# A recurrent cross-attention block and a token-mixing MLP: one fixed order for all engines in place of a scheduled order

## The chip, the cores and the metric

The kernel runs on one core of one Trainium2 chip. A core has a matrix engine (PE, with its weight loads shown as PEld), a vector engine (DVE), a scalar engine (ACT), GpSimd (POOL) and a queue engine (SP). Each works through a queue of its own in order, and engines wait for each other by semaphores. Loads and stores go through 16 DMA engines, fed from the queues of SP, ACT and POOL. Matmul results land in PSUM, which has eight banks of 2 KB per partition; DVE and ACT copy them from there to SBUF. The metric is the device time of one execution in microseconds; less is better.

## The reference

The inputs are x (8 batches, 8 heads, 512 tokens, 64 features) and a state (32 rows for each batch and head). Each head's tokens attend to its state rows, and its state rows attend to its tokens. The two results, 512 + 32 = 544 rows, go through a linear token-mixing step.

```python
scores = scale * x @ state.T;  a = softmax(scores);   xread = a @ state
scores2 = scale * state @ x.T; a2 = softmax(scores2); sread = a2 @ x
y = concatenate([xread, sread], axis=2)        # (B, H, 544, 64) -> (B, 544, 512)
wq = y @ w_q;  wk = y @ w_k                    # 512 -> 64
mixed = (scale * wq @ wk.T) @ y                # over the 544 tokens
out = maximum(mixed, 0) @ w_out                # 512 -> 512, float32
```

## The kernel before

The work is cut by batch. For each batch b the steps are these (line numbers are those of the listing at the end of this section; the names in brackets are the short names that the new order uses for the same step):

- `s_xT` (xT): 16 PE transposes of x, in two halves of 8 into `xT_ps`; DVE copies each half out (L147, L152).
- `s_pt` (pt, exp, rs, rinv, A): the scores, 16 matmuls into `pt_ps` (L161); ACT takes the exponential `E` (L169); DVE sums and inverts (L174, L176); POOL multiplies into `A` (L178).
- `s_stbd`: POOL spreads the state rows of a batch to a block-diagonal tile `stbd`, two multiplications by a mask (L190).
- `s_at` (at, ate): 8 transposes of `A`, copied to `AT` by DVE (L203, L207).
- `s_srd` (srd, sums, srn, sbd): the state's reading, 32 small matmuls of 32 output rows and 8 for the sums (L216, L226); DVE normalises to `srn`; POOL spreads it to `sbd` (L242).
- `s_srT`, `s_wqk` (srT, wq, wks, wk): the two projections, from `AT` and from `srT` (L264, L273, L285, L294), copied out as `wq` by ACT and `wk` by DVE. The products with the state, `sw`, are made once at the start (L124).
- `s_g`, `s_v` (g, v): two small contractions that leave `V` in SBUF (L310, L326, L330, L338).
- `s_mix`, `s_mix_s` (mix0, mix1, mixs): the mixing, 8 matmuls of 64 rows and 4 short ones (L348, L367); the rectified results `rmix` are written by ACT (first half, L357) and DVE (second half, L359), `rmix_s` by ACT.
- `s_fin_mm` (fin0 to fin3): the output projection, 16 matmuls of 512 columns (L382). Two quarters share one tile of two banks, which ACT copies to `ost` (L393) and SP stores. `s_fin_s` (fs) does the same for the state rows of four batches at once (L412).

The matmul tiles differ in shape: most are 128 by 128, but `srd` and the state part of `wk` have 32 output rows (128*32 in the profile's rows), `wq` has 64 (128*64), `mix` and `mixs` contract over 64 rows (64*128), and `sw` is 64*32. PE runs each shape in a tiling mode of its own.

The code is written as a pipeline of three stages over ten rounds: batch i is in its front (xT, pt, srd), batch i-1 in its middle (at, wqk, g, v), batch i-2 in mix and fin. The framework's scheduler then moves instructions within what the tile pools and dependences allow. PSUM is split into pool `psA` (three tiles of two banks) and pool `psB` (two tiles of one bank). At the start x of batch 0 is loaded as float32 by four DMAs on ACT's queue and cast on DVE and ACT; the other batches and `w_out` are loaded and cast in flight by eight DMAs that POOL issues one after the other (L88 to L92); state and `w_q`, `w_k` come on SP's queue.

Of the kernel before, what the change touches and what calls it, by code (L numbers as in the profile page):

```python
# [14 lines left out]

@with_exitstack
def kernel(
# [9 lines left out]
    nc = tc.nc  # L27

    B, H, S, D = x.shape
    NS = state.shape[2]  # L30
    DM = H * D
# [11 lines left out]
    xin = ctx.enter_context(tc.tile_pool(name="xin", bufs=1))  # L43
# [5 lines left out]
    x_bf = [xin.tile([128, H, NC * D], BF, name=f"x_bf{b}") for b in range(B)]  # L49
    x_f0 = xin.tile([128, H, NC * D], FP, name="x_f0")  # L50
    st_f = const.tile([128, B, 2, D], FP, name="st_f")
    st_bf = const.tile([128, B, 2, 2, D], BF, name="st_bf")
    stT = const.tile([128, B, H, 2, NS], BF, name="stT")
    w_f = const.tile([128, NP, 2, DH], FP, name="w_f")
# [13 lines left out]
    st_src = state.rearrange("b (r q) n d -> (q n) (b r) d", r=2)  # L68
    nc.sync.dma_start(out=st_f[:, 0], in_=st_src[:, 0:2])
# [3 lines left out]
    wsrc = [w.rearrange("(r q d) j -> r d q j", r=2, q=NP) for w in (moe_w_q, moe_w_k)]  # L73
# [5 lines left out]
    nc.gpsimd.memset(stT[:, 1:B].bitcast(FP), 0.0)  # L79
    nc.vector.memset(stT[:, 0].bitcast(FP), 0.0)  # L80
    nc.vector.memset(mask, 0.0)
    nc.vector.memset(ones, 1.0)
    nc.vector.memset(warm, 0.0)
    nc.scalar.activation(out=warm, in_=warm, func=AF.Exp)
    for q in range(NP):
        nc.vector.memset(mask[NS * q : NS * q + NS, q : q + 1], 1.0)

    nc.gpsimd.dma_start(out=x_bf[1], in_=xsrc(1, 0, H))  # L88
    for b in range(2, B):
        nc.gpsimd.dma_start(out=x_bf[b], in_=xsrc(b, 0, H))  # L90
        if b == 2:
            nc.gpsimd.dma_start(out=w_o, in_=moe_w_out.rearrange("(k p) e -> p k e", p=128))  # L92

    def setup_st(b0, b1):
        n = b1 - b0
        nc.vector.tensor_copy(  # L96
            out=st_bf[:, b0:b1],
            in_=st_f[:, b0:b1, :, None, :].to_broadcast((128, n, 2, 2, D)),
        )
        ps = psB.tile([128, n, 2, HN], BF, name="stT_ps", tag="psB")  # L100
        for b in range(b0, b1):
            for r in range(2):
                nc.tensor.transpose(  # L103
                    out=ps[:, b - b0, r, :], in_=st_bf[:, b, r, :, :], identity=ident
                )
        for b in range(b0, b1):
            for c2 in range(2):
                rows = slice(64 * c2, 64 * c2 + 64)
                src = ps[rows, b - b0].rearrange("p r (q n) -> p (r q) n", q=NP)
                if c2 == 0:  # L110
                    nc.vector.tensor_copy(out=stT[rows, b, :, c2, :], in_=src)
                else:
                    nc.scalar.copy(out=stT[rows, b, :, c2, :], in_=src)

    def setup_w():
        nc.scalar.copy(out=w_qk[:, :, 0:2, :], in_=w_f)
        nc.vector.tensor_copy(out=w_qk[:, :, 2, :], in_=w_f[:, :, 1, :])

    def setup_sw(g):
        ps = psA.tile([128, 2, B // 2, 2 * DH], FP, name="sw_ps", tag="psA")  # L120
        for bb in range(B // 2):
            for q in range(NP):
                for r in range(2):
                    nc.tensor.matmul(  # L124
                        out=ps[NS * q : NS * q + NS, r, bb, :],
                        lhsT=stT[64 * r : 64 * r + 64, g * (B // 2) + bb, NP * r + q, r, :],
                        rhs=w_qk[64 * r : 64 * r + 64, q, 0:2, :],
                        start=True,
                        stop=True,
                    )  # L130
        src = ps.rearrange("p r b j -> p b r j")
        bs = slice(g * (B // 2), (g + 1) * (B // 2))
        dst = sw[:, bs].rearrange("p b r t j -> p b r (t j)")
        if g == 0:
            nc.scalar.copy(out=dst, in_=src)
        else:
            nc.vector.tensor_copy(out=dst, in_=src)

    live = [dict() for _ in range(B)]

    def s_xT(b):
        L = live[b]
        ps = psA.tile([128, NC // 2, H, 128], BF, name="xT_ps", tag="psA")
        xT = work.tile([128, NC // 2, H, 128], BF, name="xT")
        for u in range(2):
            for h in range(H):
                nc.tensor.transpose(  # L147
                    out=ps[:, u, h, :],
                    in_=x_bf[b][:, h, 128 * u : 128 * u + 128],
                    identity=ident,  # L150
                )
            nc.vector.tensor_copy(out=xT[:, u], in_=ps[:, u])  # L152
        L["xT"] = xT

# [359 lines left out]
```

## Time and profile before

| what | before |
|---|---|
| median of three runs (lowest, highest) | 116.53 us (115.98, 117.35) |
| the profiled execution's own time | 116.32 us |
| its span in the trace | 114.5 us |
| matmuls recorded on PE | 1321 |
| read from and written to HBM | 10.22 MB, 8.91 MB |

The profiled execution lies 0.2 us under the median; 1.8 us of it lie outside the span. A busy share in the profile counts a matmul from its start until its last result has left the array. A stream of matmuls overlaps these passages, so a PE that is shown 95% busy need not be streaming all of that time. The granted clock is the share of TensorE's full speed.

### The profile page before, as it was taken

Reading aid. Unit: us, or ns where it says so; the run is one execution under the profiler, and the core shown is the slowest. Engines: PE = TensorE matmul, PEld = TensorE weight load, DVE = VectorE, ACT = ScalarE, POOL = GpSimd, SP = SyncE. Lnnn points to the kernel's source line nnn. Section 1 sums busy time; section 2 is a strip of 40 time slices with the busy share of each in tenths; the row PEclk is TensorE's granted clock in tenths of the full one; section 3 lists DMA queues with packets and bytes.
Section 4 is the critical chain, followed back from the end, with each engine's and each line's share of the span. In section 5 each row is a group of like instructions: output and inputs, shape, how many; then the busy total and the mean of one; then the engine's idle time right before and its main releaser. Section 6 shows DMA issues by size and latency. Waiting matters only on the chain. (4 is left out here: it accounts for less than half of the span.)

```text
span 114.5 us, 3055 instructions
## 1 busy us (share of the span) xinstructions
PE 87.3 (76%) x1321; PEld 54.8 (48%) x1336; DVE 58.2 (51%) x117; ACT 47.3 (41%) x70; POOL 43.3 (38%) x55
## 2 busy tenths in 40 slices
PE   0223398684979999999999989989998997949600
PEld 0002375684655657366555726565674554524200
DVE  1325565658423727852953694296449435344200
ACT  0522449030163346438442644544573454480210
POOL 8995000583990390086058107700630640000000
PEclk9999999999755999999999999999999999999995
DMA  1999999999900044040404404052332224044381
GB/s 39 290 287 183 197 204 197 199 197 198 126 0 0 6 183 182 7 186 6 183 0 189 180 3 167 24 192 77 157 154 74 104 84 183 0 203 187 87 298 48
DMA packets 14933, 15.13 MB, mean 132 GB/s; under 512 B 3656, under 2 KB 12360, under 8 KB 14920
## 3 DMA queue, kind: packets, MB, share of 16 engines
q0 software_dynamic: 7808, 4.19, 26.3%
q1 hardware_dynamic: 5736, 9.18, 22.5%
q10 hardware_dynamic: 1376, 1.57, 4.6%
q8 instruction: 10, 0.16, 0.6%
q14 instruction: 3, 0.02, 0.1%
HBM read 10.22 MB, written 8.91 MB: 167 GB/s over the span
## 5 line engine op out<-in xcount | busy, mean ns | idle before, releaser
L382 PE MATMUL fin_ps<-w_o,rmix 128*128 128x512 bf16 x113 | 32.7, 386 | 4.9 <-ACT rmix L357 2.2
L178 POOL TENSOR_TENSOR A<-E,rinv 128x1024 bf16<-128x1024 bf16 x8 | 15.3, 1912 | 47.3 <-DVE rinv L176 28.8
L393 ACT COPY ost<-fin_ps 128x1024 f32<-128x1024 f32 x14 | 14.2, 1012 | 10.8 <-PE fin_ps L382 10.4
L147 PE MATMUL xT_ps<-ident,x_bf 128*128 128x128 bf16 x128 | 13.0, 252 | 6.1 <-ACT x_bf L429 3.0
L382 PEld LDWEIGHTS <-rmix 128*128 128x128 bf16 x128 | 10.7, 99 | 14.4 <-issue 2.8
L152 DVE COPY xT<-xT_ps 128x1024 bf16<-128x1024 bf16 x16 | 11.0, 686 | 12.4 <-PE xT_ps L147 12.4
L147 PEld LDWEIGHTS <-x_bf 128*128 128x128 bf16 x128 | 9.7, 112 | 9.3 <-ACT x_bf L429 3.5
L169 ACT ACTIVATE E<-pt_ps 128x1024 bf16<-128x1024 f32 x8 | 8.2, 1023 | 11.9 <-PE pt_ps L161 11.9
L359 DVE TENSOR_SCALAR rmix<-mix_ps 128x1024 bf16<-128x1024 f32 x8 | 9.7, 1218 | 6.5 <-PE mix_ps L348 6.5
L174 DVE TENSOR_REDUCE rsum<-E 128x32 f32<-128x1024 bf16 x8 | 9.7, 1213 | 2.8 <-ACT E L169 2.8
L338 ACT ACTIVATE V<-v_ps 128x512 bf16<-128x512 f32 x8 | 4.8, 597 | 14.9 <-PE v_ps L330 14.9
L242 POOL TENSOR_TENSOR sbd<-srn,mask 128x256 bf16<-128x256 bf16 x16 | 9.5, 612 | 1.8 <-DVE srn L237 1.7
L190 POOL TENSOR_TENSOR stbd<-st_bf,mask 128x256 bf16<-128x256 bf16 x16 | 9.4, 611 | 0.0
L357 ACT ACTIVATE rmix<-mix_ps 128x1024 bf16<-128x1024 f32 x8 | 8.2, 1028 | 1.3 <-PE mix_ps L348 1.3
L103 PE MATMUL stT_ps<-ident,st_bf 128*128 128x128 bf16 x16 | 2.6, 305 | 6.9 <-DVE st_bf L96 4.0
L302 DVE CAST wk<-wk_ps 128x384 bf16<-128x384 f32 x8 | 4.4, 548 | 6.6 <-PE wk_ps L294 6.6
L348 PE MATMUL mix_ps<-wq,V 64*128 64x256 bf16 x64 | 6.7, 291 | 1.2 <-ACT V L338 0.7
L161 PE MATMUL pt_ps<-stT,xT 128*128 128x64 bf16 x128 | 6.9, 212 | 0.0
L203 PE MATMUL at_ps<-ident,A 128*128 128x128 bf16 x64 | 6.5, 244 | 0.0
L161 PEld LDWEIGHTS <-xT 128*128 128x128 bf16 x128 | 6.2, 112 | 0.4
L281 ACT CAST wq<-wq_ps 128x288 bf16<-128x288 f32 x8 | 3.2, 402 | 6.5 <-PE wq_ps L273 6.5
L90 POOL DMA_DIRECT2D x_bf<-in_x_dram x6 | 5.6, 958 | 0.0
(64 smaller groups left out, 110.1 us busy)
## 6 DMA issues: line engine op xcount, KB each, us to landing
out_dram<-ost SPq DMA_DIRECT2D x14, 512.0 KB, 2.6
x_bf<-in_x_dram POOLq DMA_DIRECT2D x7, 512.0 KB, 17.6
x_f<-in_x_dram ACTq DMA_DIRECT2D x4, 256.0 KB, 5.8
w_o<-in_moe_w_out_dram POOLq DMA_DIRECT2D x1, 512.0 KB, 13.0
out_dram<-ost_s SPq DMA_DIRECT2D x2, 256.0 KB
out_dram<-ost SPq DMA_DIRECT2D x2, 256.0 KB, 3.6
out_dram<-ost ACTq DMA_DIRECT2D x2, 256.0 KB, 4.9
st_f<-in_state_dram SPq DMA_DIRECT2D x1, 448.0 KB
```

The lines of the kernel that those rows point to most:

```text
L147: nc.tensor.transpose(out=ps[:, u, h, :], in_=x_bf[b][:, h, 128 * u : 128 * u + 128], identity=ident,)
L152: nc.vector.tensor_copy(out=xT[:, u], in_=ps[:, u])
L161: nc.tensor.matmul(out=ps[:, 2 * u : 2 * u + 2, r, NS * q : NS * q + NS], lhsT=L["xT"][:, u, h, :], rhs=stT[:, b, h, :, :], start=(h == 0) ...
L169: nc.scalar.activation(out=E.rearrange("p c r q n -> p c r (q n)"), in_=ps, func=AF.Exp, scale=float(scale))
L174: nc.vector.reduce_sum(out=rsum, in_=Ev, axis=AX.X)
L178: nc.gpsimd.tensor_tensor(out=A.rearrange("p c r q n -> p (c r q) n"), in0=Ev, in1=rinv[:, :, None].to_broadcast((128, NC * 2 * NP, NS)), ...
L190: nc.gpsimd.tensor_tensor(out=stbd[:, r], in0=st_bf[:, b, r, 0:1, :].to_broadcast((128, NP, D)), in1=mask[:, :, None].to_broadcast((128, N ...
L242: nc.gpsimd.tensor_tensor(out=sbd[:, r], in0=srn[:, r : r + 1, :].to_broadcast((128, NP, D)), in1=mask[:, :, None].to_broadcast((128, NP, D)),
L357: nc.scalar.activation(out=dst, in_=ps, func=AF.Relu)
L359: nc.vector.tensor_scalar(out=dst, in0=ps, scalar1=0.0, scalar2=None, op0=ALU.max)
L382: nc.tensor.matmul(out=L["fin"][:, c % 2, :], lhsT=rmix[:, b, k, c // 2, 128 * (c % 2) : 128 * (c % 2) + 128], rhs=w_o[:, k, :], start=(k ...
L393: nc.scalar.copy(out=L["ost"], in_=L["fin"])
```

## The change

The scheduler is switched off (`tc.manual_schedule()`), and the body becomes a table of steps: each token names a step, a batch and an engine (t PE, a ACT, v DVE, p POOL; `1` marks a fin that gets a bank of its own), and the program is emitted in that order. The table has 369 tokens; two of its lines are shown. Batches are no longer taken in strict order: the fronts of batches 0 to 3 come first, then 5, 6, 4 and 7, and the steps of several batches are interleaved.

```diff
+ORDER = """
...
+sw.1.t srn.0.v sw.0.t ix6.0.p rs1.0.v pt0.1.t swe.0.a pt1.1.t srT.0.t xT1.2.t rinv1.0.v exp0.1.a
...
+fin0.7.1 oe1.6.a fin1.7.1 oc0.7.v fin2.7.1 oc1.7.a fin3.7.1 oc2.7.v oc3.7.a
+"""
...
+    ctx.enter_context(tc.manual_schedule())
...
-    work = ctx.enter_context(tc.tile_pool(name="work", bufs=3))
-    ostp = ctx.enter_context(tc.tile_pool(name="ostp", bufs=3))
-    psA = ctx.enter_context(tc.tile_pool(name="psA", bufs=3, space=bass.MemoryType.PSUM))
-    psB = ctx.enter_context(tc.tile_pool(name="psB", bufs=2, space=bass.MemoryType.PSUM))
+    work = ctx.enter_context(tc.tile_pool(name="work", bufs=4))
+    psA = ctx.enter_context(tc.tile_pool(name="psA", bufs=2, space=bass.MemoryType.PSUM))
+    psB = ctx.enter_context(tc.tile_pool(name="psB", bufs=4, space=bass.MemoryType.PSUM))
...
     for g in range(4):
-        nc.scalar.dma_start(out=x_f0[:, 2 * g : 2 * g + 2], in_=xsrc(0, 2 * g, 2 * g + 2))
+        eng = nc.sync if g % 2 == 0 else nc.scalar
+        eng.dma_start(out=x_f0[:, 2 * g : 2 * g + 2], in_=xsrc(0, 2 * g, 2 * g + 2))
...
+    nc.gpsimd.memset(stbd.bitcast(FP), 0.0)
...
+    def st_cast(n, g, e):
+        b0, b1 = (0, 1) if g == 0 else (1, B)
+        copy(e, st_bf[:, b0:b1], st_f[:, b0:b1])
+        if g == 1:
+            for q in range(NP):
+                rows = slice(NS * q, NS * q + NS)
+                nc.sync.dma_start(
+                    out=stbd[rows, :, :, q, :].rearrange("p b r d -> p (b r) d"),
+                    in_=st_bf[rows].rearrange("p b r d -> p (b r) d"),
+                )
...
+    def pt_mm(n, b, e):
+        u = int(n[-1])
+        ps = psB.tile([128, 2, 2, HN], FP, name="pt_ps", tag="psB")
...
+    def wks_mm(n, b, e):
+        ps = psB.tile([128, NC + 2, DH], FP, name="wk_ps", tag="psB")
+        for q in range(NP):
+            for h in range(2):
+                nc.tensor.matmul(
+                    out=ps[64 * h : 64 * h + 64, NC : NC + 2, :],
+                    lhsT=L[b]["srT"][:, q, :, :],
...
+    def fin_mm(n, b, e):
+        c = int(n[-1])
+        if e == "1":
+            ps = psB.tile([128, DM], FP, name="fin1_ps", tag="psB")
...
+    for tok in ORDER.split():
+        n, b, e = tok.split(".")
+        STEP[n.rstrip("0123456789")](n, int(b), e)
```

The further parts: `pt_ps`, `xT_ps` and the exponential are handled in halves of one bank each; the copies out of PSUM go to ACT or DVE as the token says; the state part of `wk` runs in tiles of 64 output rows instead of 32 (8 matmuls instead of 16), behind `wq`, which has 64 too; the state's transposes write 64 rows each (32 instead of 16); `w_q`, `w_k` and a quarter of batch 0's x are cast by POOL, between its DMA issues; `stbd` is kept for all batches at once, zeroed by POOL and filled by four DMAs on SP's queue, so that the sixteen multiplications at L190 go. `ost` and all other work tiles have four buffers.

Three places show the new order. First POOL's queue at the start, from the identity's last instruction to the first work on results (`x_bf_74` to `x_bf_80` are batches 1 to 7). Before:

```order
masks.py:199 AFFINE_SELECT ident<-ident 128x128
L88 DMA x_bf_74<-in_x_dram 128x8x256
L90 DMA x_bf_75<-in_x_dram 128x8x256
L92 DMA w_o<-in_moe_w_out_dram 128x4x512
L90 DMA x_bf_76<-in_x_dram 128x8x256
L90 DMA x_bf_77<-in_x_dram 128x8x256
L90 DMA x_bf_78<-in_x_dram 128x8x256
L90 DMA x_bf_79<-in_x_dram 128x8x256
L90 DMA x_bf_80<-in_x_dram 128x8x256
L178 TENSOR_TENSOR A<-E,rinv 128x1024
```

After (`x_bf_69` is batch 0, `x_bf_70` to `x_bf_76` are batches 1 to 7):

```order
L124 MEMSET stbd 128x2048
L152 CAST x_bf_69<-x_f_77 128x512
L146 DMA x_bf_70<-in_x_dram 128x8x256
L146 DMA x_bf_71<-in_x_dram 128x8x256
L143 DMA w_o<-in_moe_w_out_dram 128x4x512
L146 DMA x_bf_72<-in_x_dram 128x8x256
L157 CAST w_qk<-w_f 128x4x128
L158 CAST w_qk<-w_f 128x4x64
L146 DMA x_bf_73<-in_x_dram 128x8x256
L146 DMA x_bf_74<-in_x_dram 128x8x256
L146 DMA x_bf_75<-in_x_dram 128x8x256
L345 TENSOR_TENSOR sbd<-srn,mask 128x256 x2
```

The loads now stand behind a memset and a cast that needs batch 0's first quarter, batch 4's and later ones behind the casts of `w_q` and `w_k`, and batch 7's behind the first `sbd`. Second, DVE's queue at the start, from batch 0's casts on. Before:

```order
L427 CAST x_bf_73<-x_f_81 128x512 x2
L96 CAST st_bf<-st_f 128x512 x3
L96 CAST st_bf<-st_f 128x256
L117 CAST w_qk<-w_f 128x4x64
L111 COPY stT<-stT_ps 64x8x32
L152 COPY xT<-xT_ps 128x1024
```

After:

```order
L133 CAST x_bf_69<-x_f_77 128x512 x2
L133 CAST st_bf<-st_f 128x896
L133 COPY stT<-stT_ps 64x24x32
L133 COPY stT<-stT_ps 64x32x32
L133 COPY xT_236<-xT_ps 128x1024
```

The cast of `w_qk` no longer stands ahead of the copies; batch 0's `xT` is copied by ACT, and `xT_236` is batch 1's. Third, ACT's queue in the last batch, from its last `wq` on. Before:

```order
L281 CAST wq<-wq_ps 128x288
L393 COPY ost<-fin_ps 128x1024
L338 ACTIVATE V<-v_ps 128x512
L393 COPY ost<-fin_ps 128x1024
L357 ACTIVATE rmix<-mix_ps 128x2x2x256
L374 ACTIVATE rmix_s<-mixs_ps 128x4x32
L406 COPY ost<-fin_ps 128x512
L407 DMA out_dram<-ost 128x512
```

After:

```order
L131 CAST wq<-wq_ps 128x288
L131 CAST wk<-wk_ps 128x384
L131 COPY ost<-fin_ps 128x1024
L457 ACTIVATE V<-v_ps 128x512
L131 COPY ost<-fin_ps 128x1024
L137 ACTIVATE rmix_s<-mixs_ps 128x4x32
L137 ACTIVATE rmix<-mix_ps 128x2x2x256 x2
L131 COPY ost<-fin_ps 128x1024
L131 COPY ost_1909<-fin_ps 128x512
L531 DMA out_dram<-ost_1909 128x512
```

ACT now rectifies both halves of the last mix, with copies of earlier batches' fins around them.

More of the change, by code (lines that the diff above doesn't have):

```diff
@@ L84 @@
     nc.scalar.activation(out=warm, in_=warm, func=AF.Exp)
+    nc.vector.memset(mask, 0.0)
     for q in range(NP):
         nc.vector.memset(mask[NS * q : NS * q + NS, q : q + 1], 1.0)
[L88 to L91, printed above, removed]
-            nc.gpsimd.dma_start(out=w_o, in_=moe_w_out.rearrange("(k p) e -> p k e", p=128))
[L94 to L100, printed above, removed]
+    nc.vector.memset(stT.bitcast(FP), 0.0)
@@ L101, in setup_st, with st_tr @@
+    def st_tr(n, g, e):
+        b0, b1 = SG[g]
+        ps = psB.tile([128, b1 - b0, 2, HN], BF, name="stT_ps", tag="psB")
         for b in range(b0, b1):
             for r in range(2):
[L103 to L121, printed above, removed]
+                for c2 in range(2):
+                    nc.tensor.transpose(
+                        out=ps[64 * c2 : 64 * c2 + 64, b - b0, r, :],
+                        in_=st_bf[:, b, r, :],
+                        identity=ident,
+                    )
@@ L130, in setup_sw @@
                     )
[L131 to L153, printed above, removed]
@@ L155, in s_pt @@
[L155 to L168 removed]
+        G["sw", p] = ps
@@ L172, in s_pt @@
[L172 to L181 removed]
+            out=L[b]["E"][:, 2 * u : 2 * u + 2].rearrange("p c r q n -> p c r (q n)"),
@@ L223, in s_srd, with sums @@
                     )
+        L[b]["srd"] = ps
+    def sums(n, b, e):
         for r in range(2):
```

502 lines of the change are left out of this document (274 added, 228 removed).

## The prediction

> **What bounds the kernel now.** I read the page's busy times and slices first, then the table of windows, then PE's timeline. The busy times and slices say that PE is the nearest to full, and that the end is reached through PE:
>
> ```profile
> PE 87.3 (76%) x1321; PEld 54.8 (48%) x1336; DVE 58.2 (51%) x117; ACT 47.3 (41%) x70; POOL 43.3 (38%) x55
> PE   0223398684979999999999989989998997949600
> ```
>
> From 37 us on PE is shown 90% busy or more; before that it is not. The table of windows (columns: length, busy time of PE, PEld, DVE, ACT, POOL, then PE's clock, DMA share, GB/s) splits the two regimes:
>
> ```profile
> 15.00:18.00 3.00, 3.00 (x69) 1.92 (x66) 1.41 (x5) 1.34 (x4) 0.00 (x0) 1.00 1.31 203
> ...
> 27.00:30.00 3.00, 1.74 (x76) 1.54 (x76) 1.82 (x6) 0.40 (x1) 2.24 (x2) 0.99 1.45 197
> 30.00:33.00 3.00, 2.23 (x17) 1.05 (x18) 0.88 (x4) 0.60 (x1) 3.00 (x6) 0.50 0.21 30
> 42.28:52.37 10.09, 9.58 (x156) 5.81 (x156) 6.06 (x11) 4.89 (x7) 4.18 (x6) 1.00 0.29 117
> ```
>
> The DMA engines are full (a share of 1 and more) until the loads end at about 30 us. In the middle a batch takes a round of 10.1 us. How much of that is streaming? PE's timeline of one round (start, length, step, count):
>
> ```profile
> 42.28 0.61 PE L147 MATMUL xT_ps<-ident,x_bf 128*128 128x128 bf16 x8
> 42.83 0.39 PE L348 MATMUL mix_ps<-wq,V 64*128 64x256 bf16 x4
> 43.06 0.25 PE L367 MATMUL mixs_ps<-wq,V 64*128 64x32 bf16 x4
> ...
> 44.94 0.64 PE L161 MATMUL pt_ps<-stT,xT 128*128 128x64 bf16 x16
> 45.42 0.38 PE L382 MATMUL fin_ps<-w_o,rmix 128*128 128x512 bf16 x1
> 45.85 0.22 PE L253 MATMUL srT_ps<-ident,srn 128*128 128x128 bf16 x1
> 46.30 0.82 PE L382 MATMUL fin_ps<-w_o,rmix 128*128 128x512 bf16 x3 [0.23 <-DVE rmix L359]
> 47.05 0.41 PE L264 MATMUL wq_ps<-AT,sw 128*64 128x256 bf16 x4
> 47.40 1.25 PE L382 MATMUL fin_ps<-w_o,rmix 128*128 128x512 bf16 x5
> 48.58 0.30 PE L273 MATMUL wq_ps<-srT,w_qk 128*64 128x32 bf16 x8
> 48.81 0.41 PE L285 MATMUL wk_ps<-sw,AT 128*128 128x64 bf16 x8
> 49.15 0.41 PE L294 MATMUL wk_ps<-w_qk,srT 128*32 128x128 bf16 x16
> 49.62 0.42 PE L216 MATMUL srd_ps<-x_bf,E 128*32 128x64 bf16 x32
> 49.97 0.35 PE L226 MATMUL srd_ps<-ones,E 128*128 128x1 bf16 x8
> 50.22 0.39 PE L310 MATMUL g_ps<-wk,A 128*128 128x64 bf16 x8
> ...
> 51.08 0.38 PE L326 MATMUL v_ps<-sbd,wk 128*128 128x512 bf16 x1
> ...
> 51.51 0.38 PE L330 MATMUL v_ps<-stbd,G 128*128 128x256 bf16 x2
> ```
>
> Each length holds one passage through the array, which a following group overlaps. A fin alone takes 0.38 and five take 1.25, so one streams 0.22 and the passage is 0.17. Taking 0.17 off each group gives the streaming price: half an xT 0.44, an `at` the same (8 transposes too), pt 0.47 (0.24 a half), mix 0.22 for four, mixs 0.08, srT 0.05, wq 0.24 + 0.13, wk 0.24, its state part 0.24, srd 0.25, sums 0.18, g 0.22, v 0.21 + 0.21, sixteen fins 3.46. One batch is 0.88 + 0.44 + 0.47 + 0.44 + 0.08 + 0.05 + 0.37 + 0.48 + 0.25 + 0.18 + 0.22 + 0.42 + 3.46 = 7.7 us. So 2.4 us of each 10.1 us are lost between groups, although PE looks 95% busy. Of these, part is the change of tile shape: five fins from 47.40 stream 1.08 and the next shape begins at 48.58, 0.10 late. A round changes shape 12 times, 1.2 us; the other 1.2 us are waits for data, such as the 0.23 in the row at 46.30.
>
> The start is the second place, and has two faults. DVE's and PE's timelines there:
>
> ```profile
> 12.40 0.29 DVE L117 CAST w_qk<-w_f 128x256 bf16<-128x256 f32 x1 [2.15 <-DMA w_f<-in_moe_w_k_dram]
> ...
> 12.81 0.67 DVE L152 COPY xT<-xT_ps 128x1024 bf16<-128x1024 bf16 x1
> ...
> 13.81 1.06 PE L147 MATMUL xT_ps<-ident,x_bf 128*128 128x128 bf16 x8
> ...
> 21.73 1.01 PE L147 MATMUL xT_ps<-ident,x_bf 128*128 128x128 bf16 x8 [0.87 <-DVE xT L152]
> ```
>
> The copy of batch 0's first `xT` stands on DVE behind a cast that waits for `w_f`, and PE's second `xT` comes only at 13.81. And eight transposes take 1.06 us where they later take 0.61: after the passage that is 0.89 against 0.44, half speed. The clock column shows a loss only from 30 us (0.50 above), before that the lengths are the better witness. First fin, and the end:
>
> ```profile
> 35.26 0.61 PE L382 MATMUL fin_ps<-w_o,rmix 128*128 128x512 bf16 x1
> ...
> 107.70 1.02 PE L382 MATMUL fin_ps<-w_o,rmix 128*128 128x512 bf16 x3 [0.84 <-DVE ost L403]
> 108.76 0.59 ACT L406 COPY ost<-fin_ps 128x512 f32<-128x512 f32 x1 [2.14 <-PE fin_ps L382]
> 109.37 0.36 ACTq L407 DMA_DIRECT2D out_dram<-ost  x1
> ```
>
> The last matmul ends at 108.7; a copy, a DMA issue and the DMA's landing take the remaining 5.8 us of the 114.5 us span.
>
> **The change part by part.** All streaming: eight batches 61.9, eight `fins` of 0.22 each 1.7, setup about 1.4 (64 `sw` at the price of srd's small tiles, 0.5, and 32 half-wide state transposes at xT's price halved, 0.9), in sum 65. The matmuls removed (half of `wk`'s state part) stay at 0.24, since half as many run in tiles twice as wide.
>
> *The start, to the first fin.* The first fin in the new order (batch 2's) stands behind twelve xT halves 5.3, ten pt halves 2.4, four srd with sums and srT 1.9, three `at` 1.3, three wq and wk 2.6, two g 0.4, one v and one mix 0.9, setup 1.4: 16.2 us of streaming and, by the order, 26 changes of shape, 2.6 us. PE can begin near 6 us (the row below: x's first quarter lands after 3.4 us, then a cast). But the fronts need the loads:
>
> ```profile
> DMA to landing us min/median/max: 3.4/5.8/6.5
> DMA to landing us min/median/max: 9.8/17.6/22.6
> L88 POOL DMA_DIRECT2D x_bf<-in_x_dram x1: 1060/1060/1060, 2.7 to 2.7; - x1
> L393 ACT COPY ost<-fin_ps 128x1024 f32<-128x1024 f32 x14 | 14.2, 1012 | 10.8 <-PE fin_ps L382 10.4
> L178 POOL TENSOR_TENSOR A<-E,rinv 128x1024 bf16<-128x1024 bf16 x8 | 15.3, 1912 | 47.3 <-DVE rinv L176 28.8
> L79 POOL MEMSET stT<- 128x1792 f32 x1 | 1.6, 1595 | 0.0
> ```
>
> The second row is `x_bf`; the first of its issues stands at 2.7 us (third row), so batch 1 lands at 12.5. POOL will issue it later, behind a memset of 2048 (1.8 us by the last row) and a cast of 512 elements whose price on POOL no row shows: between 0.5 (half of ACT's 1.0 for 1024 elements) and 1.0 (half of `A`'s 1.9). I take 1.0, nearest by engine; either way the issue is near 5.6 us. That costs nothing while the state, weight and batch 0 loads, moved ahead, keep the DMA engines full; if that cover were gone it would cost the 2.9 us of delay. The order of the bytes changes, their number doesn't: 0.52 MB at 197 GB/s is 2.6 us each, in the order 1, 2, `w_o`, 3, 4, 5, 6, 7, so batch 5 lands near 24 to 25.6 and the last where it did, at 30. Batch 5's xT stands on PE ahead of 6.5 us of streaming and 0.9 us of changes to the first fin: at best 31.4, by the later landing 33. The clock matters less: at half speed to 20 us, PE loses some 4 us of 16, which the wait for batch 5 mostly hides. I take the first fin at 32.5 us, 2.8 us earlier than now, but with five fronts done instead of three.
>
> *The middle.* Behind the first fin 65 - 16.2 = 48.8 us of streaming are left, and 39 of 65 changes of shape (93 before) at 0.10: 3.9. The price is between the 0.10 of the row at 48.58 and a whole passage, 0.17, which would make it 6.6 us; I keep the 0.10 that was seen. The Trainium skill, in "TensorEngine Tiling (Array Packing)", Tiling Modes, says that a change of mode drains the array; by that rule the whole passage would be paid and the total would be 2.7 us longer, and the trace agrees only in part.
>
> *Waits.* Before, from the first fin to the last matmul were 73.5 us; of these 55.7 streamed (65 less 9.3 for three fronts, the first batch's middle and the setup, done by then) and 74 changes took 7.4, so about 10 us were waits. The new order puts other batches' fins where a step must wait. In the last batch, where the copy to `rmix` and a blocked PSUM tile cost 0.84 in the row at 107.70, it has `fins`, a mix and eight fins: 0.9 + 0.2 + 1.7 = 2.8 us, against mixs, two rectifications and their semaphores of about 2.5. Between the last batch's pt and `at` (half an exponential and half a sum, 0.5 and 0.6 by ACT's row and the one below, an inverse, `A` 1.9: some 3.4 with the semaphores) it has 3.7 us of PE work. These covers are tight: a single late step stalls the whole queue behind it. Bounds for all waits are 0 and the 10 us of before; I take 2.5, nearer the low end since most chains have a cover of their own length.
>
> *Other engines.* The rows beside ACT's 1.0 us for 1024 elements:
>
> ```profile
> L152 DVE COPY xT<-xT_ps 128x1024 bf16<-128x1024 bf16 x16 | 11.0, 686 | 12.4 <-PE xT_ps L147 12.4
> L174 DVE TENSOR_REDUCE rsum<-E 128x32 f32<-128x1024 bf16 x8 | 9.7, 1213 | 2.8 <-ACT E L169 2.8
> L190 POOL TENSOR_TENSOR stbd<-st_bf,mask 128x256 bf16<-128x256 bf16 x16 | 9.4, 611 | 0.0
> ```
>
> ACT takes ten of sixteen `xT` copies and half of the `rmix` work that DVE had, and gives up six output copies. ACT's 47 us become about 60; DVE gives up ten copies of 0.7 and more, takes the six and some small ones, and stays near 56: two thirds of the new time, so neither bounds, but each copy can be late by one instruction. The halved exponentials and sums add instructions there, hidden behind PE. POOL loses the 9.4 us of `stbd`, which were on no path. The four DMAs that replace them wait on SP's queue for the state's cast; behind them stands only the first output, at 33 us or later, and `stbd` is first needed by v near 28 us. I price them at nothing; without that cover they would cost once a landing like the 5.8 us of x's first loads. Batch 7's load stands behind the first `sbd`, near 17 us, when three other loads are still queued: nothing.
>
> *Sum.* First fin 32.5 + streaming 48.8 + shapes 3.9 + waits 2.5 + end 5.8 + outside the span 1.8 = 95.3. The profiled execution's own time is 116.3 by the same count, 0.2 under the median; I say 95.5 us.
>
> **The rivals.**
> A, the waits stay: the queues block in turn as often as now, 10 us of waits instead of 2.5, or the clock stays at half to 30 us and the first fin slips to 37. For it speaks that the order was fixed ahead and every queue is strict; 103 us, with both 107.
> B, the start goes better: batch 5 lands at 24, waits are near 1 and the clock is up early: 31.4 + 48.8 + 3.9 + 1 + 7.6 = 92.7, and 91 if `x_bf` lands quicker without batch 0's loads beside it. The Trainium skill, in "TensorE: Matmul & The Clock Gate", Part 1: The HAM clock gate, says that the clock rises after some 3.4 us of sustained work. Here PE was shown fully busy from 15 to 18 us and was still at half speed at 21.7 us, so I don't count on it.
> C, slower: with four tiles of one bank rotating through all steps, PE may pause so often that the clock falls back to half in the middle, as it did at 30 us after a thin stretch. Each us of streaming then costs another us, so from 95.5 to 117.7 it takes 22 us of streaming at half speed, 44 us of the run. Against it: from 37 to 109 us the pauses of now, as many, cost no clock. The same page's section on queue depth cycling describes this loss for bank-cycled matmuls; the trace's middle shows none.
> D, it doesn't do what it says: the copies on ACT and DVE are late throughout, the 2.4 us a batch return, and the start is bound by loads: 116, no change.
>
> **How the numbers follow.** My case (waits 0 to 5, first fin 31 to 34) 0.55, giving 92.5 to 99.5; A 0.22; B 0.15; C 0.05; D 0.03. The range reaches over A's first half and B: 90.5 to 106. About 1% is what a measurement of this kernel can tell from no change. Faster 0.92, same 0.03, slower 0.05.
>
> **What would show it.** The first fin between 31 and 34 us; batch 5's xT waiting for its load; 65 changes of shape at about 0.1; PE's waits after the first fin under 5 us in sum; clock 1.00 from the first fin on; ACT near 60 us busy. The forecast is wrong if a queue's head blocks PE for several us in the middle, or the clock column shows 0.50 after 35 us.

## The result, and the profile after

The changed kernel takes 99.44 us (median of 4 runs, 99.12 to 100.31) against 116.33 us (115.98 to 117.35) for the kernel before: a ratio of 0.855, 95% interval 0.847 to 0.863. The forecast was 95.5 us, with 90.5 to 106 as its range. Executions more than 1.5% above the fastest of their kernel are left out of the medians and ranges of the experiments below.

| us | before | after | forecast |
|---|---|---|---|
| the profiled execution's own time | 116.32 | 99.58 | 95.3 |
| first fin matmul starts | 35.26 | 37.12 | 32.5 |
| from there to the end of the last matmul | 73.5 | 53.8 | 55.2 |
| from there to the end of the span | 5.8 | 6.9 | 5.8 |

So the middle gained 19.7 us, more than the whole 16.7 us; the start gave 1.9 us back and the end 1.1. The page of the changed kernel shows the same two regimes (busy times, 40 slices, DMA packets, the costliest group):

```profile
PE 79.4 (81%) x1288; PEld 52.1 (53%) x1288; DVE 54.8 (56%) x107; ACT 57.3 (59%) x84; POOL 35.2 (36%) x42
PE   0137969486989699999999999999999999999100
PEclk9999999997599999999999999999999999999995
...
DMA packets 17044, 15.39 MB, mean 157 GB/s; under 512 B 5768, under 2 KB 14472, under 8 KB 17032
...
L505 PE MATMUL fin_ps<-w_o,rmix 128*128 128x512 bf16 x128 | 30.0, 379 | 0.0
```

From the first fin to the end of the last matmul no slice falls under 90%, and the 128 fin matmuls waited for nothing. The table of PE's waits (waited for: sum, times, longest; its first five rows) says the same, since PE's timeline has each of its waits ahead of the first fin:

```profile
PE stT_ps L179 <- DVE st_bf L133: 4.2, 2, 3.7
PE xT_ps L221 <- DMA x_bf<-in_x_dram: 2.4, 3, 1.2
PE xT_ps L221 <- POOL x_bf L152: 1.6, 1, 1.6
PE at_ps L295 <- DVE A L282: 0.8, 1, 0.8
PE at_ps L295 <- issue: 0.8, 1, 0.8
...
```

PE's timeline has the three loads it waited for (batches 1, 3 and 5), a pause without a releaser ("issue"), and the two ends of the middle:

```profile
13.15 1.89 PE L221 MATMUL xT_ps<-ident,x_bf 128*128 128x128 bf16 x16 [1.16 <-DMA x_bf<-in_x_dram]
...
22.95 1.59 PE L221 MATMUL xT_ps<-ident,x_bf 128*128 128x128 bf16 x16 [0.81 <-DMA x_bf<-in_x_dram]
...
28.33 1.07 PE L221 MATMUL xT_ps<-ident,x_bf 128*128 128x128 bf16 x16 [0.46 <-DMA x_bf<-in_x_dram]
...
32.95 0.40 PE L295 MATMUL at_ps<-ident,A 128*128 128x128 bf16 x4 [0.83 <-issue]
...
36.67 0.61 PE L221 MATMUL xT_ps<-ident,x_bf 128*128 128x128 bf16 x8
37.12 1.89 PE L505 MATMUL fin_ps<-w_o,rmix 128*128 128x512 bf16 x8
...
85.53 5.35 PE L505 MATMUL fin_ps<-w_o,rmix 128*128 128x512 bf16 x24
```

Batch 5's load, on which the forecast hung the start, came at 28.3 us and not at 24 to 25.6. Between batch 1 (13.15) and batch 3 (22.95) three loads landed, 3.3 us each; between batch 3 and batch 5 two, 2.7 us each. SP's queue and the table of windows (length, PE busy, granted clock, DMA share, GB/s) show what stood beside the slow ones:

```profile
9.09 5.25 SPq L168 DMA_DIRECT2D stbd<-st_bf  x4
```

```profile
15.00:18.00 3.00, 2.60 (x99) 1.00 1.49 215
18.00:21.00 3.00, 1.87 (x63) 1.00 1.77 215
...
24.00:27.00 3.00, 3.00 (x83) 0.55 1.46 200
27.00:30.00 3.00, 2.54 (x95) 1.00 1.45 197
```

The four `stbd` DMAs were issued from 9 to 14 us and took 10.7 us to land (median). They are the 2111 packets that the changed kernel has more than the 14933 of before; all are under 512 bytes. In 18 to 21 us, while they run, the DMA share is 1.77 instead of some 1.45, at no more GB/s than in the window before. In 24 to 27 us the granted clock is 0.55.

The end, on ACT:

```profile
92.28 0.59 ACT L131 COPY ost<-fin_ps 128x512 f32<-128x512 f32 x1 [2.50 <-DMA out_dram<-ost]
92.90 0.36 ACTq L531 DMA_DIRECT2D out_dram<-ost  x1
```

The last copy waits 2.5 us for an earlier store: the pool has four `ost1` buffers, and the last batch and the state rows need more.

### The profile page after: what moved, and what is told of

Its sections match the earlier page's. It is cut to its first block, busy times and chain, and to the rows that moved or that the text cites. A ratio compares the mean times of both kernels' runs of the same rounds, so it can differ in the third digit from the quotient of the medians.

```text
span 97.8 us, 2951 instructions
## 1 busy us (share of the span) xinstructions
PE 79.4 (81%) x1288; PEld 52.1 (53%) x1288; DVE 54.8 (56%) x107; ACT 57.3 (59%) x84; POOL 35.2 (36%) x42
## 4 chain that ended last, share of the span: by engine, by line
PE 56%; DMA 26%; SPq 6%; POOL 2%; ACT 2%; issue 2%; DVE 1%; ACTq 0%; POOLq 0%
PE fin_ps L505 22%; DMA x_bf<-in_x_dram 13%; DMA w_f<-in_moe_w_k_dram 7%; DMA out_dram<-ost 6%; PE mix_ps L471 5%; SPq L114 4%; PE xT_ps L221 4%; PE at_ps L295 4%; PE wq_ps L371 2%; PE wk_ps L409 2%; PE pt_ps L237 2%; PE g_ps L425 2%; PE v_ps L440 2%; PE fins_ps L505 2%; PE srd_ps L308 2%; PE v_ps L444 2%
## 5 line engine op out<-in xcount | busy, mean ns | idle before, releaser
L282 POOL TENSOR_TENSOR A<-E,rinv 128x1024 bf16<-128x1024 bf16 (+1 forms) x8 | 14.5, 1816 | 23.9 <-DVE rinv L276 23.8
L131 ACT COPY ost<-fin_ps 128x1024 f32<-128x1024 f32 (+1 forms) x10 | 9.3, 928 | 9.8 <-PE fin_ps L505 5.7
L133 DVE COPY ost<-fin_ps 128x1024 f32<-128x1024 f32 (+1 forms) x8 | 8.7, 1092 | 11.1 <-PE fin_ps L505 11.1
L137 ACT ACTIVATE rmix<-mix_ps 128x1024 bf16<-128x1024 f32 x12 | 12.2, 1024 | 4.7 <-PE mix_ps L471 4.7
L345 POOL TENSOR_TENSOR sbd<-srn,mask 128x256 bf16<-128x256 bf16 x16 | 9.5, 617 | 10.4 <-DVE srn L335 5.7
L131 ACT COPY xT<-xT_ps 128x1024 bf16<-128x1024 bf16 x10 | 9.8, 1014 | 4.8 <-PE xT_ps L221 4.7
L253 ACT ACTIVATE E<-pt_ps 128x512 bf16<-128x512 f32 x16 | 9.2, 597 | 5.4 <-PE pt_ps L237 4.8
L268 DVE TENSOR_REDUCE rsum<-E 128x16 f32<-128x512 bf16 x16 | 10.5, 674 | 1.3 <-ACT E L253 1.3
L133 DVE COPY xT<-xT_ps 128x1024 bf16<-128x1024 bf16 x6 | 4.0, 688 | 4.8 <-PE xT_ps L221 4.8
L139 DVE TENSOR_SCALAR rmix<-mix_ps 128x1024 bf16<-128x1024 f32 x4 | 4.9, 1222 | 0.9 <-PE mix_ps L471 0.9
L295 PEld LDWEIGHTS <-A 128*128 128x128 bf16 x64 | 3.9, 98 | 2.4 <-issue 1.2
```

Of the source, the lines that this page charges most:

```text
L131: nc.scalar.copy(out=out, in_=in_)
L133: nc.vector.tensor_copy(out=out, in_=in_)
L137: nc.scalar.activation(out=out, in_=in_, func=AF.Relu)
L253: nc.scalar.activation(out=L[b]["E"][:, 2 * u : 2 * u + 2].rearrange("p c r q n -> p c r (q n)"), in_=L[b][f"pt{u}"], func=AF.Exp, scale=f ...
L268: nc.vector.reduce_sum(out=L[b]["rsum"][:, w], in_=L[b]["E"].rearrange("p c r q n -> p (c r q) n")[:, w], axis=AX.X,)
L282: eng.tensor_tensor(out=L[b]["A"].rearrange("p c r q n -> p (c r q) n")[:, w], in0=L[b]["E"].rearrange("p c r q n -> p (c r q) n")[:, w], ...
```

## The experiments

Times are medians of 4 runs, less those left out as said above. The kernel before ran beside each of three groups, with 116.86, 116.35 and 116.57 us as its medians. The changed kernel ran again in the second group (beside `modes`, `pipe` and `all3`) and in the third (beside `beforew`, `pipe32` and `all4`); `tail`, `stbd`, `wo` and `warm` are of the first group and had no such control. Differences under about 1 us between groups are not told apart.

### The changed kernel again

> The changed kernel again, as the measure for the other kernels of this job: 99.4 us, first fin at 37.1 us, 53.8 us from there to the end of the last matmul, 6.9 us behind it.

> The changed kernel again, beside the others: 98.8 to 99.6 us by either theory; it is what all4 is held against.

99.01 us (98.88 to 99.32; first fin 36.32, middle 53.8) and 98.71 us (98.53 to 99.35; first fin 36.83, middle 53.8). The first fin itself scatters by 0.8 us.

### What a change of tile shape costs

The matmuls of `wq` and `wk`, of different shapes, are interleaved; the same matmuls run, with 114 changes of shape in place of 65.

```diff
-        for r in range(2):
-            for h in range(2):
...
+        for c in range(NC):
+            for o, l, r_, st, sp in jobs[3 * c : 3 * c + 3]:
+                nc.tensor.matmul(out=o, lhsT=l, rhs=r_, start=st, stop=sp)
+            for r in range(2):
...
+                    out=L[b]["wkp"][:, c, :],
```

> The changed kernel with the matmuls of wq and wk of a batch alternating in groups of three and two (the state part of wk ahead of them), the same matmuls on the same data: 114 changes of shape instead of 65, six more in each batch, 30 of the 49 behind the first fin. Theory 'a change costs 0.10 us': 3.0 us more behind the first fin and up to 1.9 us before it, 102.4 to 104.3 us. Rival 'a change costs a whole passage, 0.17 us': 5.1 us and up to 3.2 us, 104.5 to 107.7 us. Rival 'changes cost nothing, waits did': 99.4 us.

105.19 us (104.57 to 105.72), 6.2 us more than the control, over 49 changes 0.126 us each. PE's timeline in this run has the alternation:

```profile
67.20 0.23 PE L387 MATMUL wq_ps<-srT,w_qk 128*64 128x32 bf16 x3
67.37 0.23 PE L389 MATMUL wk_ps<-sw,AT 128*128 128x64 bf16 x2
67.53 0.23 PE L387 MATMUL wq_ps<-srT,w_qk 128*64 128x32 bf16 x3
67.70 0.23 PE L389 MATMUL wk_ps<-sw,AT 128*128 128x64 bf16 x2
```

A group of two or three small matmuls occupies PE for 0.17 us where it streams 0.04 to 0.06. In the middle (first fin at 39.44, last matmul's end at 96.98: 57.5 us, 3.8 more than the control) stand five of the eight batches, so 30 of the 49: again 0.126 each. PE's timeline shows no wait in the middle; the price is paid at the changes. It is the change of shape and not the new output tile: in the changed kernel's timeline above eight `xT` transposes (36.67) are followed by fins into another tile, of the same shape, 0.45 us later, and eight transposes stream for 0.44. By PE's start times in the changed kernel itself, its 39 changes in the middle cost 0.06 to 0.16 us each, 4.5 us in sum, so 0.115 on average; the two ways of measuring agree within a tenth.

### The tiles and pools without the fixed order

The changed kernel's tiles, pools, loads, halves and POOL casts, but in before's three-stage order and with its split between ACT and DVE; the scheduler is on. It changes shape 71 times.

```diff
-    ctx.enter_context(tc.manual_schedule())
...
-stc.0.v stt.0.t xc0.0.p ste.0.v stf.0.a xc1.0.a ix1.0.p xc2.0.v ix2.0.p xc3.0.v xT0.0.t iwo.0.p
+stc.0.v stt.0.t ste.0.v stf.0.a ix1.0.p ix2.0.p iwo.0.p ix3.0.p ix4.0.p ix5.0.p ix6.0.p ix7.0.p
...
```

> The changed kernel's tiles, pools, loads and halved steps, but with the steps written in the old three-stage order on the engines they had before, and the scheduler on: 71 changes of shape. Theory 'the order fills the waits': the waits behind the first fin return to some 10 us from 1 us, less the changes of shape that stay away; 108 us (104 to 114). Rival 'the tiles and pools gave the gain': 100 us. Rival 'the two PSUM tiles of two banks are too few without the order': over 114 us.

103.95 us (103.84 to 104.85): 12.4 us of the gain stay. The other 4.9 are what the order is worth, together with the new split between ACT and DVE and the scheduler switched off, which this run does not separate. The first fin comes at 29.3 us, with three fronts done, and the last matmul ends at 95.6. PE's waits, of which the last of these rows lies in the middle:

```profile
...
PE xT_ps L219 <- DVE x_bf L131: 2.6, 2, 1.4
PE pt_ps L235 <- DVE xT L131: 2.5, 1, 2.5
PE at_ps L293 <- POOL A L280: 1.7, 1, 1.7
PE mix_ps L469 <- ACT ost L129: 0.7, 1, 0.7
...
```

With 55.7 us of streaming behind the first fin (the prediction's figure for three fronts) and 57 of the 71 changes there at 0.126 (7.2), the middle's 66.4 us leave 3.5 us for waits and gaps. The timeline shows 1.5 us of it as three waits (it lists those from about 0.15 us on), where before's middle has ten with 4.7 us and the changed kernel's has none.

### The number of one-bank tiles

The kernel of the last run with before's split of PSUM: three tiles of two banks and two tiles of one bank, in place of two and four (the expectation's text names these numbers wrongly; its times stand).

```diff
-    psA = ctx.enter_context(tc.tile_pool(name="psA", bufs=2, space=bass.MemoryType.PSUM))
-    psB = ctx.enter_context(tc.tile_pool(name="psB", bufs=4, space=bass.MemoryType.PSUM))
+    psA = ctx.enter_context(tc.tile_pool(name="psA", bufs=3, space=bass.MemoryType.PSUM))
+    psB = ctx.enter_context(tc.tile_pool(name="psB", bufs=2, space=bass.MemoryType.PSUM))
```

> The kernel of the run pipe (the changed kernel's tiles, loads and halves in before's three-stage order), with three and two buffers in the two small PSUM pools in place of four and three, as before had. Theory: the larger number of one-bank tiles is what took most of the waits out of the middle; with the old number the stretch from the first fin group to the last matmul grows from 66.4 to 70 us or more, and the time is 107 to 110 us. Rival: the waits went with the shorter queues on ACT and DVE (casts on POOL, halves), the number of buffers is idle; the time is 103.5 to 105 us.

107.9 us (107.61 to 108.67), 4.0 us more. The middle (29.79 to 98.37) takes 68.6 us, 2.2 more, though this build changes shape only 42 times there, 15 fewer: at 0.126 that is 1.9 less, so waits and gaps grew by some 4 us. The timeline's waits in the middle are now 13, with 5.2 us in place of 1.5. The profiled runs differ by 2.8 us, since that of the kernel with four tiles was the slowest of its four. PE's waits now have rows for tiles of other steps that are not yet copied out, `at` behind `xT` and `g` behind `wk`:

```profile
PE fin_ps L503 <- ACT rmix L135: 2.3, 2, 1.4
...
PE at_ps L293 <- DVE xT L131: 1.6, 5, 0.4
PE g_ps L423 <- DVE wk L131: 1.2, 6, 0.2
```

### The start fault, undone in the kernel before

```diff
-        nc.scalar.copy(out=w_qk[:, :, 0:2, :], in_=w_f)
-        nc.vector.tensor_copy(out=w_qk[:, :, 2, :], in_=w_f[:, :, 1, :])
+        nc.gpsimd.tensor_copy(out=w_qk[:, :, 0:2, :], in_=w_f)
+        nc.gpsimd.tensor_copy(out=w_qk[:, :, 2, :], in_=w_f[:, :, 1, :])
```

> The kernel before, with the two casts of w_q and w_k on POOL in place of ACT and DVE; nothing else. Theory (the prediction's start fault): in before the copies of the first batch stand behind these casts, which wait for a load, so that PE starts late; with the casts on POOL the first fin group comes 3 to 5 us earlier than at 35.3 us, the stretch from there to the last matmul stays at 73 to 75 us, and the time is 111.5 to 114 us. Rival: the loads set the start in any case (as they did in the run with warm-up matmuls), so the first fin group comes at 34 to 36 us, and the time stays at 115.5 to 117.5 us.

112.94 us (112.71 to 113.03), ratio 0.967 (0.960 to 0.973): 3.6 us from two lines. PE's timeline has the second half of batch 0's transposes at 11.54 us, where before had it at 13.81, and the first fin 2.5 us earlier:

```profile
11.54 1.06 PE L147 MATMUL xT_ps<-ident,x_bf 128*128 128x128 bf16 x8
...
32.72 1.04 PE L382 MATMUL fin_ps<-w_o,rmix 128*128 128x512 bf16 x4
```

The fault was real: a cast that waits for a load, with a copy that PE needs behind it in DVE's queue. The first fin moved by less than the expected 3 to 5 us; the rest of the gain lies behind it.

### What holds the changed kernel's start

Five runs. The state spread by four POOL copies (4.3 us) in place of the DMAs:

```diff
...
-                nc.sync.dma_start(
+            nc.gpsimd.tensor_copy(
                 out=stbd[rows, :, :, q, :].rearrange("p b r d -> p (b r) d"),
```

> The changed kernel with the block-diagonal state spread by four POOL copies, 32 partitions each, in the time in which POOL waits for the weights, instead of four DMAs of 2048 packets of 128 bytes. Theory 'loads set the start': the packets took DMA time from the batch loads; batch 3 lands near 21 us instead of 22.9, batch 5 near 26.5 instead of 28.3, PE's waits of 0.8 and 0.5 us for them go, the first fin begins about 1.3 us earlier, 98.0 us (97.0 to 98.6). Rival 'clock or dependences set the start': loads earlier, first fin where it was, 99.4 us.

`w_out` loaded behind batch 7 instead of ahead of batch 3:

```diff
-stc.0.v stt.0.t xc0.0.p ste.0.v stf.0.a xc1.0.a ix1.0.p xc2.0.v ix2.0.p xc3.0.v xT0.0.t iwo.0.p
+stc.0.v stt.0.t xc0.0.p ste.0.v stf.0.a xc1.0.a ix1.0.p xc2.0.v ix2.0.p xc3.0.v xT0.0.t
...
-srTe.0.v sbd.0.p rinv0.0.v xT0.2.t A0.0.v exp1.1.a xTe1.2.a rs0.1.v ix7.0.p at0.0.t srd.1.t ste.2.v
+srTe.0.v sbd.0.p rinv0.0.v xT0.2.t A0.0.v exp1.1.a xTe1.2.a rs0.1.v ix7.0.p iwo.0.p at0.0.t srd.1.t ste.2.v
```

> The changed kernel with the output weights loaded after batch 7 instead of after batch 2. Theory 'loads set the start': batches 3 to 7 land 2.7 to 3.5 us earlier, PE's waits of 0.8 and 0.5 us go, first fin about 1.3 us earlier (up to 2.5 if the clock then stays at full speed), 98.0 us. Rival 'clock or dependences set the start': no change of the first fin, 99.4 us. Third case: the weights land after 37 us and the first fin waits for them, over 100 us.

Ten matmuls of 512 columns ahead of and between the first state transposes, whose result nothing reads:

```diff
+        for _ in range(k):
+            nc.tensor.matmul(out=ps, lhsT=wz[:, 0:128], rhs=wz, start=True, stop=True)
```

> The changed kernel with ten additional matmuls of 512 columns on constants, six ahead of the first state transposes and four behind them, whose results nothing reads: they only keep PE busy while it waits for data. Theory 'loads set the start': transposes of batch 0 run at full speed, PE then waits longer for batches 1, 3 and 5, first fin within 0.5 us of 37.1, 99.4 us (98.9 to 99.6). Rival 'the clock sets the start': the half-speed stretches to 17 us and from 22.7 to 26.7 us shrink, first fin 2 to 4 us earlier, 96 to 97.5 us.

And these three with six output buffers as well (the run with the buffers alone is below), without and with the ten matmuls:

> The changed kernel with its state spread on POOL, the output weights loaded last, and six output buffers. Theory 'loads set the start, the sum adds': first fin at 35.5 us or earlier, 97.2 us (96.5 to 97.8). Rival 'something else takes over': PE's unexplained pauses of 0.3 to 1.2 us between 20 and 33 us, which stand exactly 256 PE instructions apart (448, 704, 960), stay or grow, and the stores at the end take the time that the copy gains: 98.3 us, no better than the state's spreading alone.

> The run all3 (six output buffers, state spread by POOL copies, w_o loaded behind batch 7) with the ten warm-up matmuls of the run warm. Theory: with no load to wait for, the half clock of the first 17 us is what is left at the start; the warm-up takes 1 us or more out of the first fin group's 36.6 us, and the time is 96.8 to 97.6 us. Rival: the loads, or PE's pauses while they run, still set the start; the first fin group stays at 36 to 37 us and the time at 98.0 to 98.6 us.

| run | us | first fin at |
|---|---|---|
| state by POOL | 98.25 (97.97 to 98.67) | 36.56 |
| `w_out` last | 98.81 (98.69 to 99.01) | 35.87 |
| warm-up | 99.00 (98.63 to 99.55) | 37.07 |
| buffers, state by POOL and `w_out` last | 98.28 (98.09 to 98.52) | 36.59 |
| the same with the warm-up | 98.62 (98.32 to 99.64) | 36.61 |

The first fin came at most 0.5 us ahead of the earlier of the two controls. With the state by POOL the waits for batches 3 and 5 are gone, and a pause without a releaser stands in their place:

```profile
PE sw_ps L202 <- issue: 1.0, 1, 1.0
...
PE xT_ps L222 <- DMA x_bf<-in_x_dram: 0.4, 1, 0.4
```

The loads themselves gained little. By issue and time to landing, batch 5's landed at 27.5 us in this run and at 27.8 to 28.5 in the six runs that have the DMAs and the same order of loads; from batch 1 to batch 3 a load took 3.0 us, against 3.1 to 3.4 with the DMAs and 2.6 in the kernel before. The run of the fourth row goes further: batch 5's load, issued at 15.7 us, lands 8.7 us later, at 24.4, within the forecast. Its view and PE's timeline:

```profile
L147 POOL DMA_DIRECT2D x_bf<-in_x_dram x1: 883/883/883, 15.7 to 15.7; - x1
DMA to landing us min/median/max: 8.7/8.7/8.7
...
27.61 1.90 PE L223 MATMUL xT_ps<-ident,x_bf 128*128 128x128 bf16 x16
```

Batch 5's transposes begin 3.2 us behind the landing and wait for nothing, and the first fin is at 36.59 all the same.

With the warm-up the rate was up near 7 us (eight `pt` matmuls take 0.41 us at 9.54, where the changed kernel's at 9.85 take 0.61). Then PE waited longer for the loads, and the rate fell back: the granted clock (third figure of the windows' row) is 0.50 in 24 to 27 us and as low in the next 3 us:

```profile
9.54 0.41 PE L244 MATMUL pt_ps<-stT,xT 128*128 128x64 bf16 x8
...
12.88 1.34 PE L228 MATMUL xT_ps<-ident,x_bf 128*128 128x128 bf16 x16 [2.03 <-DMA x_bf<-in_x_dram]
...
24.00:27.00 3.00, 3.00 (x87) 0.50 1.46 197
```

With both, the last run of the table, PE's waits behind its first matmul sum to 7.4 us, no less than the 6.5 us of the same kernel without the ten matmuls:

```profile
PE at_ps L304 <- issue: 2.0, 1, 2.0
...
PE at_ps L304 <- POOL A L291: 1.4, 1, 1.4
PE stT_ps L188 <- DVE st_bf L136: 1.2, 1, 1.2
PE xT_ps L230 <- DVE x_bf L136: 0.8, 1, 0.8
PE wq_ps L389 <- issue: 0.6, 1, 0.6
```

So no edit moved the first fin clear of the controls' scatter. Early loads alone do not: other waits and the pauses took their place. What the start would be at the full rate is open, since no run held the clock up: it is 0.50 in 24 to 30 us with the warm-up, and 0.50 in 12 to 15 us in the last run of the table.

The combination of three ran below all runs of its own control (98.52 at most, against 98.88 at least), 0.7 us in the medians, but not by its start, which came 0.3 us later than the control's. The gain stands behind the last store. In the five kernels without the `stbd` DMAs (the two before-kernels among them) the program ends 1.0 us after that store has landed, in the nine with them 1.6 to 1.8 us after. That is shown by place in all fourteen traces; why the DMAs lengthen the close of the program is not.

### The wait at the end

```diff
+    ost1p = ctx.enter_context(tc.tile_pool(name="ost1p", bufs=6))
...
-        ost = work.tile([128, DM], FP, name="ost1")
+        ost = ost1p.tile([128, DM], FP, name="ost1")
```

> The changed kernel with six buffers instead of four for the 512-column output tiles (ost1). Theory 'tail': in the changed kernel the last copy waits for the store of an earlier output tile in the same buffer (2.5 us shown, of which 1.4 us lie behind the last matmul); with a buffer of its own it starts right after the last matmul, 98.0 us instead of 99.4. Rival: the stores at the end are limited by the DMA engines, and the copy only moves the wait into the store: 99.4 us, and the last store lands later after its issue than 4 us.

98.83 us (98.65 to 99.02), within what can be told the time of the two controls. The wait went, on ACT:

```profile
90.40 0.59 ACT L132 COPY ost<-fin_ps 128x512 f32<-128x512 f32 x1 [1.14 <-PE fin_ps L506]
91.02 0.36 ACTq L532 DMA_DIRECT2D out_dram<-ost  x1
```

But the last store, issued 1.9 us earlier, took 6.2 us to the end of the span (97.2) instead of 4.9. From the last matmul to the end are 6.8 us against 6.9, and the last store lands 5.1 us behind the last matmul in both: the stores that are still queued set its landing, not the buffer.

## Why the prediction was right, and where it was not

The sign and the range were right. The sum of 95.3 lies 4.3 us under the profiled execution: the start's +4.6, the middle's -1.4 and the end's +1.1. That 99.44 still falls into the forecast's own case (92.5 to 99.5) is luck in part, since the first fin, at 37.1, lies outside its 31 to 34 and the middle made up for some of it.

*The middle: right mechanism, two terms off in opposite directions.* Streaming 48.8 and 39 changes at the measured 0.126 (4.9) make 53.7 of the 53.8 us, which leaves about 0.1 us for waits where 2.5 was taken. The term for changes was low (0.10 against 0.126). The 0.17 of a whole passage, which the Trainium skill's rule in "TensorEngine Tiling (Array Packing)", Tiling Modes, would have made it, was high: the run with interleaved shapes lies between. By the same price the middle of before was 55.7 of streaming, 9.6 of changes (76 in its timeline; the forecast counted 74) and 8.2 of waits and other gaps (about 10 in the forecast); the timeline shows 4.7 of these as waits, the rest is too short for it. The 19.7 us won there are 6.9 of streaming that was moved ahead of the first fin, 4.7 of changes and 8.1 of waits and gaps. The tight covers that the forecast feared (last batch, `pt` to `at`) held.

*The start: the step that failed.* The forecast said that batch 5's load lands near 24 to 25.6 us, that the first fin follows 7.4 us behind it, and that the wait for this load mostly hides what the half clock costs. None of the three held.

The load landed at 28.3. Counting 2.6 us for each load was short from the outset: in the kernel before, the same load, issued at 7.2 us, landed at 26.5, and the last one at 31.8 and not at 30. The sentence on the four `stbd` DMAs, "I price them at nothing", is a smaller part: only the place where their result is first read was checked, not the DMA engines that they share with the loads, and without them batch 5 landed 0.3 to 1.0 us earlier. What else slowed the loads beside them is not shown. By place, the DMAs did cost time where nobody looked, some 0.7 us at the close of the program.

But this load does not set the first fin. Where it landed at 24.4, within the forecast, the first fin still came at 36.59. What was mis-sized is PE's own time. The waits of the changed kernel ahead of the first fin sum to 11.1 us by its table, so PE was at work for 26.0 of the 37.1 us, where the forecast has 16.2 + 2.6 = 18.8. Dearer changes are 0.7 of the difference; the rest, some 6 us, is mostly work at less than the full rate, such as the 16 transposes of 1.89 us at 13.15 (1.07 at 28.33) and the clock of 0.55 in 24 to 27 us. The forecast put this loss at some 4 us and hid it behind batch 5's wait, which was 0.5 us long. In the run where that load is early PE is at work just as long (10.4 us of waits, 26.2 of work). Of the 8.8 us from batch 5's transposes to the first fin, instead of 7.4, 0.8 is the pause at 32.95; dearer changes are 0.2.

*The start: the part that was right.* The cast ahead of batch 0's copy was a fault, worth 3.6 us in the kernel before. The new start brings the first fin to 29.3 us in the old order, 6.0 us earlier; the new order then spends this, and 1.9 us more, on two further fronts and 6.9 us of streaming ahead of the first fin.

*The clock.* The forecast set the Trainium skill's 3.4 us of sustained work ("TensorE: Matmul & The Clock Gate", Part 1: The HAM clock gate) aside, because PE was shown fully busy from 15 to 18 us and was still slow. The traces bear it out that a time since the last wait does not tell here when the rate rises. In the kernel before, PE's timeline has no listed wait from 13.43 to 18.1 us, 4.7 us, and the transposes at 21.73 are still slow. By the spacing of the transposes (0.107 us at the half rate, 0.056 at the full one) and the lengths of the groups behind them, the rate rose some 3.3 us behind the wait ahead of 13.15 in the changed kernel, 1.4 us behind the one ahead of 12.78 in its first repeat, and 5 to 6 us behind the first matmul of the warm-up run, in which PE has no listed wait from 1.46 us on. A return of the half rate changed little: the first repeat has one (clock 0.50 in 21 to 24 us) and its first fin at 36.32, the second has none and 36.83.

*The end.* The term 5.8 was taken from before. In the changed kernel the last 24 fins run without a gap, so the outputs of 1.5 batches reach the store queue together, and the last store lands 5.1 us behind the last matmul instead of 4.8. The close of the program behind it takes 1.8 us instead of 1.0, with the `stbd` DMAs as said above; together 6.9.

*Other points.* ACT's busy time is 57.3 us (60 forecast), DVE's 54.8 (56). The POOL cast of 512 elements, taken as 1.0, is 0.61. Rival A named 37 us for the first fin, by a half clock to 30 us. The first fin did slip there and work at the half rate is a large part of it, but the rate was up from 16.5 to 23.3 us and again from 26.7, and A's waits did not come. Rival C's half clock in the middle did not come: the slices show 9 from 28 us on.

What the parts are worth, by the runs: tiles, pools, halves and the new start 12.4 us (116.35 to 103.95), of which four one-bank tiles in place of two are about 4.0 (in the old order); the order by hand, with its split between ACT and DVE, 4.9 us (to 99.01), of which fewer changes of shape cannot be more than 0.8 (six at 0.126); most of the rest is the 3.5 us of waits and gaps in the middle.

## What to carry to other kernels

Where PE shows 95% busy, price a round by its streaming and by its changes of tile shape (some 0.12 us each here); what is left is waits and gaps, and more small PSUM tiles took half of these before any order was written by hand. A DMA that nobody waits for soon is not free: the four here held a load up by 0.3 to 1.0 us and, by place, the program's close by some 0.7. A late load is not by itself what sets a start: add up how long the engine behind it is at work, at the rate that it has there, before calling any of that hidden. Taking away one limit of this start showed only the next, so a forecast should not subtract one alone.

## What the runs showed of the hardware that was not expected

While loads fill the DMA engines, PE pauses without any releaser at fixed counts of its own matmuls. Counted in PE's timeline, 223, 351 or 479 matmuls stand ahead of every such pause, 15 of them in nine traces of the changed kernel and its variants (the warm-up run has none); these numbers are 128 matmuls apart, and with their weight loads 256 instructions. The second repeat of the changed kernel, and then the last run of the table, which has ten matmuls more at the start; both rows stand behind 351 matmuls:

```profile
26.48 0.30 PE L201 MATMUL sw_ps<-w_qk,stT 64*32 64x128 bf16 x15 [0.78 <-issue]
```

```profile
25.71 0.18 PE L389 MATMUL wq_ps<-srT,w_qk 128*64 128x32 bf16 x1 [0.55 <-issue]
```

The extra matmuls moved the pause to earlier work, not to an earlier count. So it goes with the instruction stream and not with a step. The page has ten packets and 0.16 MB for instruction queue q8, 16 KB each, and the DMA records show one packet to each pause: all 15 pauses end 2.3 to 2.5 us after such a packet has started. For the changed kernel's pause that ends at 32.95 it is this one, from the DMA view of 30.4 to 30.5 us:

```profile
q8 instruction: 1, 0.02, 55.8%
```

That the pauses are waits for PE's next instructions fits this closely, but no run tested it. What the loads have to do with it is open: the packets take some 0.9 to 1.0 us beside the loads, and most take as long behind them. The pauses are 0.2 to 2.0 us long, and none is seen behind 33 us, when the loads have ended.

The multiplication into `A` over half a batch took 1.70 us on DVE, where POOL took 1.14 for the same shape in the same run, as the view of that line shows:

```profile
L282 POOL TENSOR_TENSOR A<-E,rinv x8: 1142/1912/1914, 19.1 to 72.0; 128x1024 bf16<-128x1024 bf16 x7, 128x512 bf16<-128x512 bf16 x1
L282 DVE TENSOR_TENSOR A<-E,rinv x1: 1700/1700/1700, 17.6 to 17.6; 128x512 bf16<-128x512 bf16 x1
```
